# Opening of a fused LayerNorm, linear-attention and gated MLP kernel: idle products, the split of one load, and the order of a few products

## Chip, cores, metric

One core of one Trainium2 chip. The metric is the device time of one execution in microseconds; lower is better. A kernel is run several times, medians of fast runs are quoted, and executions of one kernel mostly differ by some tenths of a microsecond (those of before lay between 220.24 and 222.91 in all). "Landed" is the moment at which the profile has the last completion signal of a transfer.

## The reference

S = 2048 tokens of width 640, 32 heads of 20, MLP width 1728, all bf16:

```python
xn = layernorm(x)
q, k, v = split(xn @ wqkv)
pq, pk = phi(q), phi(k)                  # phi(t) = where(t > 0, t + 1, exp(t)) + 1e-6
o = (pq @ (pk^T v)) / (pq . sum(pk) + 1e-6)
s = o @ wo
g = silu(relu(xn @ w1) @ w2)
out = x + s * g
```

## The kernel before

The kernel is scheduled by hand: every operation is appended to the program of one engine (PE is TensorE, DVE VectorE, ACT ScalarE, POOL GpSimd, SP the queue of most transfers), and a small scheduler puts in the semaphore waits. Each engine is given its operations in the order in which they were appended, and the timelines below show PE, DVE and ACT starting them in that order. x comes in 16 tiles of 128 tokens. Only the opening, tiles 0 to 3, matters here. These tiles are centred by DVE (a mean half made by ACT, half by DVE, or all by ACT), transposed on PE, copied from PSUM to SBUF by DVE and ACT, and multiplied with the K columns of A_wqkv. `wqk` has five row pieces; `wk_load(k0, k1)` fetches pieces k0 to k1-1, and `K_mm(t, b, k0, k1)` appends the products of tile t with those pieces, two products of 320 columns per piece.

```python
zero = nc.alloc_sbuf_tensor("zero", [P, P], bf)
# [...]
sc.op("DVE", lambda eng: eng.memset(zero[:, :], 0.0), W=[("zero",)])
# [...]
x_load(0)                    # SP queue, 160 KB
x_load(1, 1, "ACT")          # ACT queue
wk_load(0, 2)                # SP, pieces one and two, 320 KB
x_load(2, 2, "ACT")          # ACT, tiles 2 and 3 in one transfer
wk_load(2, 3)                # SP, piece three, 160 KB
wk_load(3, 5)                # SP, pieces four and five
w1_load(0, "SP")
# [...]
def fill(n):                 # "idle products": their result is never read
    sc.group("PE", [(lambda eng: eng.matmul(ps[7][:, 0:P], lhsT=zero[:], rhs=zero[:], start=True, stop=True))
                    for _ in range(n)], R=[("zero",)], W=[("ps", 7)])
fill(31)
# [...]  the opening, in the order of each engine's program
bn(0, 0)                     # DVE, statistics of half of tile 0
mean_act(0, HN)              # ACT
half_mean_dve(0)
centre(0)                    # DVE
mean_act(1, 0)
transposes(0, 0)             # PE, five of 128x128
xcT_copy(0, 0, 0, "DVE")
centre(1)
fill(5)
K_mm(0, 2, 0, 1)             # tile 0, piece one
transposes(1, 6)
xcT_copy(0, 0, 1, "DVE")
bn(0, 1)                     # DVE, needed only for the scale used much later
mean_act(2, 0)               # ACT, waits for tile 2
xcT_copy(1, 6, 0, "DVE")
xcT_copy(1, 6, 1, "ACT")
K_mm(0, 2, 1, 3)             # tile 0, pieces two and three
K_mm(1, 4, 0, KA)            # tile 1, pieces one and two (KA = 2)
centre(2)
transposes(2, 0)
mean_act(3, HN)
bn(3, 0)
# [...]
K_mm(1, 4, 2, 3); K_mm(2, 6, 0, KA); K_mm(2, 6, 2, 3)
transposes(3, 0)
# [...]  22 more K products, then H blocks (products of 512 columns with w1)
```

## Time and profile before

| | before |
|---|---|
| median of the first 3 runs (range) | 220.86 us (220.54 to 221.12) |
| span of the profiled run | 219.3 us |
| PE busy | 214.5 us, 98% of the span |
| PE waits named in the whole span | 1.0 us, 0.6 us, 0.2 us |

The page gives the busy time of each engine with its share of the span, and the chain of work that ended last:

```profile
PE 214.5 (98%) x1451; PEld 133.7 (61%) x1461; DVE 119.1 (54%) x219; ACT 84.2 (38%) x140; POOL 43.8 (20%) x69
...
PE 95%; DMA 2%; DVE 1%; issue 0%; SPq 0%; ACT 0%; DVEq 0%
```

PE is the bound, and all other engines have room. What PE waited for, in total us, number of times and longest:

```profile
PE psT L384 <- DVE zero L356: 1.0, 1, 1.0
PE psT L493 <- DMA reg<-in_A_wqkv_dram: 0.6, 1, 0.6
PE psT L568 <- issue: 0.2, 1, 0.2
```

The second wait lies in the opening. PE's timeline there (start, length, line, how many, and in brackets the idle time before and what ended it; L384 are idle products, L468 transposes, L493 K products, L568 the H blocks):

```profile
1.04 3.49 PE L384 MATMUL psT<-zero 128*128 128x128 bf16 x31 [1.04 <-DVE zero L356]
4.43 0.79 PE L468 MATMUL psT<-ident,reg 128*128 128x128 bf16 x5
5.02 0.68 PE L384 MATMUL psT<-zero 128*128 128x128 bf16 x5
5.69 0.43 PE L493 MATMUL psT<-reg,regX 128*128 128x320 bf16 x2
5.96 0.44 PE L468 MATMUL psT<-ident,reg 128*128 128x128 bf16 x5
6.95 1.25 PE L493 MATMUL psT<-reg,regX 128*128 128x320 bf16 x8 [0.55 <-DMA reg<-in_A_wqkv_dram]
8.04 0.44 PE L468 MATMUL psT<-ident,reg 128*128 128x128 bf16 x5
8.31 1.37 PE L493 MATMUL psT<-reg,regX 128*128 128x320 bf16 x8
9.52 0.44 PE L468 MATMUL psT<-ident,reg 128*128 128x128 bf16 x5
9.80 3.15 PE L493 MATMUL psT<-reg,regX 128*128 128x320 bf16 x22
13.00 0.38 PE L568 MATMUL psT<-regX,reg 128*128 128x512 bf16 x1
```

The rate of the clock can be read from the spacing. The 31 idle products of 128 columns end at 4.53, 0.107 us apart; the five transposes that start at 5.96 are 0.056 us apart. The clock is at half rate first and is released at about 5.5 us. (The page's clock row shows full speed from the first slice on; the spacing says otherwise.) PE stands from about 6.40 to 6.95, and the chain says for what:

```profile
1.71 5.11 DMA reg<-in_A_wqkv_dram
6.82 0.14 issue
6.95 1.25 PE psT L493 x8
8.20 0.28 PE psT L468 x5
```

The third weight piece was issued at 1.71 and landed at 6.81. Tiles 2 and 3: ACT's timeline shows it idle for them until 6.45:

```profile
6.45 0.74 ACT L447 ACTIVATE regE<-reg 128x640 bf16<-128x640 bf16 x1 [1.92 <-DMA reg<-in_A_x_dram]
```

### The profile page before, as it was taken

The page shows a single profiled execution, that of the slowest core. Times are in us where ns is not written, and L with a number is a line of the kernel's source. Part 1 is how long each engine was busy: PE and PEld are TensorE (multiplying, and loading weights), DVE is VectorE, ACT ScalarE, POOL GpSimd, SP SyncE. Part 2 cuts the span into 40 slices and gives each one's busy share as a digit, 9 for nine tenths or more (in the row PEclk, how much of TensorE's full clock was granted, in tenths as well). Part 3 has the DMA queues.
Part 4 walks back from the last instruction along what each step waited for, and adds up shares of the span by engine and source line. Part 5 has one row for each costly group of instructions (what it writes and reads, how often), then busy time and mean ns, then how long its engine had stood idle before and what let it go on. Part 6 is the DMA issues. An engine that isn't in the chain of part 4 may idle for free.

```text
span 219.3 us, 3543 instructions
## 1 busy us (share of the span) xinstructions
PE 214.5 (98%) x1451; PEld 133.7 (61%) x1461; DVE 119.1 (54%) x219; ACT 84.2 (38%) x140; POOL 43.8 (20%) x69
## 2 busy tenths in 40 slices
PE   8899999999999999999999999999999999999995
PEld 7655554555545555444467777677767776777674
DVE  3798957789639999783702116930424240403134
ACT  5597675566665676554420000551021102110211
POOL 2178601120041699950000000000000000000001
PEclk9999999999999999999999999999999999999999
DMA  6977496711001243000099969932110100001011
GB/s 198 370 233 165 105 303 60 205 30 30 3 1 33 57 103 109 0 0 3 2 209 301 373 220 364 374 106 64 37 53 33 60 30 33 30 30 64 0 60 60
DMA packets 28421, 24.72 MB, mean 113 GB/s; under 512 B 12021, under 2 KB 27765, under 8 KB 28405
## 3 DMA queue, kind: packets, MB, share of 16 engines
q1 hardware_dynamic: 24677, 19.77, 31.7%
q10 hardware_dynamic: 3728, 4.73, 6.3%
q8 instruction: 11, 0.18, 0.4%
q14 instruction: 5, 0.04, 0.1%
HBM read 15.81 MB, written 5.24 MB: 96 GB/s over the span
## 4 chain that ended last, share of the span: by engine, by line
PE 95%; DMA 2%; DVE 1%; issue 0%; SPq 0%; ACT 0%; DVEq 0%
PE psT L849 26%; PE psT L568 25%; PE psT L493 10%; PE psT L789 10%; PE psT L546 10%; PE psT L900 9%; DMA reg<-in_A_wqkv_dram 2%; PE psT L867 1%; PE psT L587 1%; PE psT L819 1%; PE psT L804 1%; PE psT L676 0%; DVE reg L888 0%; ACT reg L877 0%; PE psT L468 0%
## 5 line engine op out<-in xcount | busy, mean ns | idle before, releaser
L849 PE MATMUL psT<-reg,hT 128*128 128x320 bf16 x416 | 60.5, 299 | 0.0
L849 PEld LDWEIGHTS psT<-reg,hT 128*128 128x128 bf16 x416 | 40.3, 98 | 16.4 <-issue 1.1
L568 PE MATMUL psT<-reg 128*128 128x512 bf16 x192 | 45.5, 379 | 0.3 <-issue 0.2
L888 DVE TENSOR_TENSOR reg<-psT,reg 128x640 bf16<-128x640 f32 (+2 forms) x18 | 13.3, 749 | 48.3 <-PE psT L900 47.1
L572 ACT ACTIVATE hT<-psT 128x512 bf16<-128x512 f32 x52 | 30.8, 602 | 18.0 <-PE psT L568 18.0
L568 PEld LDWEIGHTS psT<-reg 128*128 128x128 bf16 x195 | 18.9, 98 | 21.8 <-issue 0.4
L877 ACT ACTIVATE reg<-psT 128x640 bf16<-128x640 f32 x12 | 8.2, 702 | 44.7 <-PE psT L849 25.3
L893 POOL TENSOR_TENSOR reg<-reg 128x224 bf16<-128x224 bf16 x1 | 0.6, 606 | 120.3 <-DVE reg L888 120.3
L900 PE MATMUL psT<-reg,pqT 128*128 128x320 bf16 (+2 forms) x165 | 24.4, 295 | 0.0
L504 POOL TENSOR_TENSOR zacc<-zacc,reg 128x640 f32<-128x640 f32 x16 | 23.8, 1488 | 2.3 <-DVE reg L528 1.3
L546 PE MATMUL psT<-reg 128*128 128x512 bf16 x95 | 23.8, 379 | 0.3
L789 PE MATMUL psT<-reg 128*128 128x320 bf16 x160 | 21.9, 299 | 0.0
L900 PEld LDWEIGHTS psT<-reg,pqT 128*128 128x128 bf16 x165 | 16.1, 98 | 5.8
L789 PEld LDWEIGHTS psT<-reg 128*128 128x128 bf16 x160 | 15.7, 98 | 6.2
L510 ACT ACTIVATE regE<-psT 128x640 bf16<-128x640 f32 x24 | 15.6, 701 | 9.1 <-PE psT L493 9.1
L493 PE MATMUL psT<-reg 128*128 128x320 bf16 x120 | 18.3, 299 | 0.0
L554 DVE TENSOR_SCALAR regE<-psT 128x512 bf16<-128x512 f32 x20 | 13.6, 680 | 8.2 <-ACT regE L553 8.2
L556 DVE SCALAR_TENSOR_TENSOR pqT<-regE 128x512 bf16<-128x512 bf16 x20 | 17.4, 868 | 0.7
L546 PEld LDWEIGHTS psT<-reg 128*128 128x128 bf16 x100 | 9.8, 98 | 11.6
L493 PEld LDWEIGHTS psT<-reg 128*128 128x128 bf16 x120 | 11.7, 98 | 6.5 <-DMA reg<-reg 0.2
L794 DVE CAST reg<-psT 128x640 bf16<-128x640 f32 x5 | 4.1, 824 | 20.9 <-PE psT L789 20.9
L413 DVE BATCH_NORM_STATS2 stats<-reg 128x6 f32<-128x320 bf16 x32 | 14.1, 475 | 2.3 <-DMA reg<-in_A_x_dram 2.3
(69 smaller groups left out, 174.7 us busy)
## 6 DMA issues: line engine op xcount, KB each, us to landing
scr<-regE SPq DMA_DIRECT2D x4, 640.0 KB, 11.3
reg<-in_A_x_dram SPq DMA_DIRECT2D x4, 640.0 KB, 8.8
out_dram<-reg SPq DMA_DIRECT2D x15, 160.0 KB, 1.8
reg<-in_A_x_dram SPq DMA_DIRECT2D x13, 160.0 KB, 3.3
regE<-scr SPq DMA_DIRECT2D x4, 512.0 KB, 5.2
reg<-in_B_w_dram ACTq DMA_DIRECT2D x1, 1120.0 KB, 12.0
reg<-in_B_w_dram ACTq DMA_DIRECT2D x1, 1040.0 KB, 5.4
reg<-in_A_wo_dram SPq DMA_DIRECT2D x6, 160.0 KB, 4.6
```

The lines of the kernel that those rows point to most:

```text
L413: sc.op("DVE", lambda eng: eng.bn_stats(stats[:, t, a, :], xv[:, HN * a:HN * (a + 1)]), R=[("xin", t % XR)], W=[("stats", t, a)])
L493: fns.append(lambda eng, a=a, k=k, lhs=lhs: eng.matmul(ps[b + a][:, 0:HN], lhsT=lhs[:, k, tok(t)], rhs=wqk[:, k, D + HN * a:D + HN * (a + 1)],
L504: sc.op("POOL", lambda eng: eng.tensor_tensor(out=zacc[:, :], in0=zacc[:, :], in1=pk[:, t, :], op=ALU.add), R=[("zacc",), ("pk", t)], W=[( ...
L510: sc.op("ACT", lambda eng: eng.activation(out=o_.rearrange("p (a n) -> p a n", a=2), in_=ps2(b, HN), func=func, scale=scale), R=[("ps", b) ...
L546: sc.group("PE", [(lambda eng, k=k: eng.matmul(ps[b], lhsT=wqk[:, k, P * f:P * (f + 1)], rhs=xnT[:, k, schunk(j)], start=(k == 0), stop=(k ...
L554: sc.op("DVE", lambda eng: eng.tensor_scalar(out=r_, in0=ps[b], scalar1=0.0, scalar2=1e-6, op0=ALU.max, op1=ALU.add), R=[("ps", b), ("er_e ...
L556: sc.op("DVE", lambda eng: eng.scalar_tensor_tensor(out=pqT[:, f, schunk(j)], in0=e_, scalar=1.0, in1=r_, op0=ALU.min, op1=ALU.add), R=[(" ...
L568: a = sc.group("PE", [(lambda eng, k=k: eng.matmul(ps[b], lhsT=w1_sb[:, k, P * f:P * (f + 1)], rhs=src[:, k, :], start=(k == 0), stop=(k = ...
L572: sc.op("ACT", lambda eng: eng.activation(out=hT[:, f, schunk(j)], in_=ps[b], func=ACTF.Relu), R=[("ps", b)], W=[("hT", j, f)])
L789: fns.append(lambda eng, t=t, a=a: eng.matmul(ps[b + a][:, 0:HN], lhsT=xn[:, t, P * k:P * (k + 1)], rhs=pk[:, t, HN * a:HN * (a + 1)], sta ...
L849: sc.group("PE", [(lambda eng, f=f: eng.matmul(ps[b][:, 0:HN], lhsT=hT[:, f, tok(t)], rhs=w2_sb[:, f, HN * n:HN * (n + 1)], start=(f == 0 ...
L900: sc.group("PE", [(lambda eng, c=c: eng.matmul(ps[b][:, 0:hi - lo], lhsT=pqT[:, c, tok(t)], rhs=wf[:, c, lo:hi], start=(c == 0), stop=(c = ...
```

## The change

The intent is to fill the opening. Idle products read a constant that the framework sets up ahead of the program, so PE need not wait for DVE's memset. Tile 2 is loaded without tile 3, which goes behind the third weight piece on the other queue. The products with the third piece go behind four products that do not need it. The diff, whole:

```diff
-    zero = nc.alloc_sbuf_tensor("zero", [P, P], bf)
+    zero = nc.alloc_sbuf_tensor("zero", [P, 1], bf)
+    one = nc.const_aps.tensor(1.0, (P, P), bf)
@@
     x_load(0)
     x_load(1, 1, "ACT")
     wk_load(0, 2)
-    x_load(2, 2, "ACT")
+    x_load(2, 1, "ACT")
     wk_load(2, 3)
+    x_load(3)
     wk_load(3, 5)
@@
     def fill(n):
-        sc.group("PE", [(lambda eng: eng.matmul(ps[7][:, 0:P], lhsT=zero[:], rhs=zero[:], start=True, stop=True))
-                        for _ in range(n)], R=[("zero",)], W=[("ps", 7)])
+        sc.group("PE", [(lambda eng: eng.matmul(ps[7][:, 0:P], lhsT=one, rhs=one, start=True, stop=True))
+                        for _ in range(n)], W=[("ps", 7)])
@@
-    fill(31)
+    fill(32)
@@
     centre(1)
-    fill(5)
+    fill(3)
     K_mm(0, 2, 0, 1)
@@
-    K_mm(0, 2, 1, 3)
+    K_mm(0, 2, 1, KA)
     K_mm(1, 4, 0, KA)
+    K_mm(0, 2, 2, 3)
     centre(2)
```

## The prediction

> **What bounds the kernel now.** TensorE. The page's busy table gives PE 98% of a 219.3 us span, and the chain that ended last is PE for 95%. The waits of PE name three: 1.0 us at the start for the memset of `zero`, 0.55 us for a piece of A_wqkv before the matmuls at 6.95 us, and 0.2 us of issue. From 14 us on PE waits for no other engine. So only the first 9 us can change, and time saved there goes through whole to the end.
>
> **The opening, from the timeline.** The entry barrier ends at 0.72 us; the 31 idle products start at 1.04, 0.107 us apart, the cold clock's rate. K products of 320 columns come 0.136 us apart once warm, the first at 5.69. (The page's clock row shows full speed from the start; the spacing does not agree, and I trust the spacing.) Transposes of tile 0 start at 4.43, released by DVE's centring, not by the idle products. Five more idle products end at 5.55, where the first weight pieces also land, so tile 0's K products start at 5.69. PE stands from 6.40 to 6.95 for the third weight piece, landed 6.81; x tiles 2 and 3, one transfer, land at 6.42, and ACT had idled 1.92 us for them.
>
> **What the change does.**
> 1. Idle products start about 0.26 us earlier (0.78) and, being 32, end about 0.15 us earlier. Tile 0 is not ready before 4.43, so nothing is gained directly. The Trainium skill ("TensorE: Matmul & The Clock Gate", Part 1) says the clock is released by a busy window of about 3.4 us that runs free of the kernel; the earlier start moves the warm moment earlier by at most that 0.26 us on average. This trace agrees: warm about 4.4 us after the first product.
> 2. The x transfer on ACT's queue is halved. The skill ("DMA: Bandwidth & Descriptors", Queues, rings and completion order) says each engine takes packets of the queues in turn. At the 300 GB/s of the windows at 2 to 5 us, the 164 KB moved behind the third piece are 0.5 us: I estimate first two pieces at 5.2 (5.55), third at 5.8 to 6.2 (6.81), tile 2 near 5, tile 3 still near 6.4, pieces four and five unchanged near 7.6.
> 3. Two idle products fewer: 0.2 us of PE, which the earlier landing lets count.
> 4. Products that need the third piece go behind four that don't: the 0.55 us gap shrinks to at most 0.25, now for DVE's copy of tile 1.
>
> Walking the order again with these durations, the transposes of tile 3 start near 8.7 instead of 9.52: 0.6 to 0.9 us, all on PE's chain. Later needs keep margin: first part of w1 landed 9.39, needed about 12.2; transposed tile 4 landed 17.65, needed about 18.4.
>
> **Prediction.** 220.86 - 0.75 = 220.1 us, 8 in 10 between 219.4 and 220.7. Faster by over 2%: 0.01; within 2%: 0.98; slower: 0.01.
>
> **Signs.** PE's wait for A_wqkv gone or below 0.2 us; the first H block (512-column products) starts near 12.2 instead of 13.0; ACT's 1.92 us wait for x near 0.4; busy sums otherwise as before; PE still waits for nothing from 14 us on.
>
> **What would make it wrong.** A warm moment later relative to the start: the products at 5.4 to 7 us would run at half rate and the gain shrink or vanish. Tile 3 landing after 7.2 would hold DVE and ACT, which work in order. Reading a broadcast constant could be slower than a full tile. A later margin smaller than I read.

## The result

| | before | after |
|---|---|---|
| median of 6 runs (range) | 220.84 us (220.54 to 221.12) | 219.88 us (219.58 to 220.45) |
| span of the profiled run | 219.3 us | 218.3 us |
| PE busy | 214.5 us | 214.1 us |
| third weight piece landed | 6.81 us | 5.82 us |
| tile 2 landed | 6.42 us (with tile 3) | 5.22 us |
| transposes of tile 2 start | 8.03 us | 7.00 us |

The ratio is 0.9961 with a 95% interval of 0.9945 to 0.9976. A ratio here is the mean time of one kernel's fast runs over the mean of the other's fast runs of the same rounds, so it is not quite the ratio of the medians. The medians differ by 0.96 us.

The profile after, in the same views. The page:

```profile
PE 214.1 (98%) x1450; PEld 133.1 (61%) x1460; DVE 118.9 (54%) x219; ACT 84.2 (39%) x140; POOL 43.7 (20%) x69
...
PE 97%; DVE 1%; issue 0%; ACT 0%; DVEq 0%
```

PE's waits. The one for A_wqkv is gone; the first is only the entry barrier:

```profile
PE psT L386 <- PEq L994: 0.8, 1, 0.8
PE psT L570 <- issue: 0.2, 1, 0.2
```

PE's timeline (L386 idle products, L470 transposes, L495 K products, L570 H blocks):

```profile
0.82 3.57 PE L386 MATMUL psT<-const-bfloat16-1.0 128*128 128x128 bf16 x32 [0.82 <-PEq L994]
4.25 0.65 PE L470 MATMUL psT<-ident,reg 128*128 128x128 bf16 x5
4.73 0.34 PE L386 MATMUL psT<-const-bfloat16-1.0 128*128 128x128 bf16 x3
5.03 0.45 PE L495 MATMUL psT<-reg,regX 128*128 128x320 bf16 x2
5.33 0.45 PE L470 MATMUL psT<-ident,reg 128*128 128x128 bf16 x5
5.62 1.55 PE L495 MATMUL psT<-reg,regX 128*128 128x320 bf16 x8
7.01 0.44 PE L470 MATMUL psT<-ident,reg 128*128 128x128 bf16 x5
7.29 1.37 PE L495 MATMUL psT<-reg,regX 128*128 128x320 bf16 x8
8.49 0.44 PE L470 MATMUL psT<-ident,reg 128*128 128x128 bf16 x5
8.77 3.15 PE L495 MATMUL psT<-reg,regX 128*128 128x320 bf16 x22
11.98 1.46 PE L570 MATMUL psT<-regX,reg 128*128 128x512 bf16 x6
```

The idle products start at 0.82 instead of 1.04. The transposes of tile 1 start 0.63 us earlier (5.33), the K products that had stood at 6.95 start at 5.62, the transposes of tile 2 are 1.03 us earlier (7.01), and from there every line is earlier by 1.02 or 1.03 us. The gain is complete at 7 us, and nothing is given back later. (Some times in the tables are cut after the second decimal where the views round, so that a view can read 0.01 us more.) Not all of it need be the change: tile 0, whose transfer was not touched, landed at 3.04 us in this profile and at 3.23 in that of before, and over all profiles at 3.04 to 3.29. In all of them its transposes start 1.20 to 1.22 us after it landed, so 0.18 us of the 0.63 us for tile 1 was there before (4.43 to 4.25). ACT had idled 1.92 us for tile 2; it now idles 0.90:

```profile
5.24 0.74 ACT L449 ACTIVATE regE<-reg 128x640 bf16<-128x640 bf16 x1 [0.90 <-DMA reg<-in_A_x_dram]
```

PE still stands about 0.3 us inside its group of eight at 5.62: the second product starts at 5.75 and takes 0.136, the third starts at 6.18. The chain names DVE, whose statistics (L415) stand ahead of the copy that PE needs (L480):

```profile
5.53 0.40 DVE stats L415
5.93 0.20 DVE regX L480
...
6.18 0.99 PE psT L495 x6
```

### The profile page after: what moved, and what is told of

Same layout as the page of the kernel before. It is cut to its first block, busy times and chain, and to the rows that moved or that the text cites. A ratio compares the mean times of both kernels' runs of the same rounds, so it can differ in the third digit from the quotient of the medians.

```text
span 218.3 us, 3541 instructions
## 1 busy us (share of the span) xinstructions
PE 214.1 (98%) x1450; PEld 133.1 (61%) x1460; DVE 118.9 (54%) x219; ACT 84.2 (39%) x140; POOL 43.7 (20%) x69
## 3 DMA queue, kind: packets, MB, share of 16 engines
HBM read 15.81 MB, written 5.24 MB: 96 GB/s over the span
## 4 chain that ended last, share of the span: by engine, by line
PE 97%; DVE 1%; issue 0%; ACT 0%; DVEq 0%
PE psT L852 26%; PE psT L570 26%; PE psT L792 10%; PE psT L495 10%; PE psT L548 10%; PE psT L903 9%; PE psT L386 2%; PE psT L870 1%; PE psT L589 1%; PE psT L822 1%; PE psT L807 1%; PE psT L679 0%; DVE reg L891 0%; PE psT L470 0%; DVE regX L480 0%
## 5 line engine op out<-in xcount | busy, mean ns | idle before, releaser
L570 PE MATMUL psT<-reg 128*128 128x512 bf16 x192 | 45.5, 379 | 0.3 <-issue 0.2
L570 PEld LDWEIGHTS psT<-reg 128*128 128x128 bf16 x195 | 18.9, 98 | 21.9 <-issue 0.4
L495 PE MATMUL psT<-reg 128*128 128x320 bf16 x120 | 18.3, 299 | 0.0
L495 PEld LDWEIGHTS psT<-reg 128*128 128x128 bf16 x120 | 11.7, 98 | 6.5 <-DMA reg<-reg 0.2
L555 ACT ACTIVATE regE<-psT 128x512 bf16<-128x512 f32 x20 | 11.9, 597 | 8.8 <-PE psT L548 8.8
```

The costliest lines, as they stand in the source:

```text
L495: fns.append(lambda eng, a=a, k=k, lhs=lhs: eng.matmul(ps[b + a][:, 0:HN], lhsT=lhs[:, k, tok(t)], rhs=wqk[:, k, D + HN * a:D + HN * (a + 1)],
L570: a = sc.group("PE", [(lambda eng, k=k: eng.matmul(ps[b], lhsT=w1_sb[:, k, P * f:P * (f + 1)], rhs=src[:, k, :], start=(k == 0), stop=(k = ...
```

## The experiments

The gain lies in one pair of profiles, and in that pair several things differ: the landings, the place of the idle products, the order, and also the moment when the clock was released (about 5.5 before, 4.6 after). My theory, called the transfer theory, is that the landings of the third piece and of tile 2 held the opening and that splitting the load moved them. Its rivals: the clock theory (idle products from the first instruction release the clock earlier) and the order theory (moving the products fills PE's hole). Ten more kernels, and both kernels once again, were run in three calls, each call on one chip, beside the kernel before. All gave correct results.

One reading serves all: the start of the transposes of tile 3. In all fourteen profiles, the time of the run less that start lies between 211.03 and 211.10 us. So nothing after that point depends on what was changed, and each microsecond of the opening is a microsecond of the result. (I first used the first H block for this, and some of the expectations below name it. That was a poor mark: the trace of before has 192 products of that line against 195 weight loads, and in the early profiles the first product of the first H block is among the missing records, so that its start reads 0.2 us too late. The constant of 207.54 to 207.61 in an expectation below became 207.76 to 207.83 where the record was there.)

In the table, times are us from the start of the span. "Released" is the moment when 128-column products go from 0.107 to 0.056 us apart or 320-column ones from 0.267 to 0.136. "T" is the start of the transposes.

| kernel | pieces 1-2 landed | piece 3 | tile 2 | released | T tile 1 | T tile 2 | T tile 3 | that run, us |
|---|---|---|---|---|---|---|---|---|
| before | 5.55 | 6.81 | 6.42 | 5.5 | 5.96 | 8.03 | 9.52 | 220.57 |
| before, second profile | 4.80 | 7.31 | 7.48 | 6.7 to 7.4 | 6.11 | 8.81 | 10.30 | 221.33 |
| order only | 4.75 | 6.06 | 6.35 | 5.6 | 5.83 | 7.68 | 9.17 | 220.21 |
| idle products only | 5.29 | 6.58 | 6.13 | 5.7 | 5.90 | 7.80 | 9.29 | 220.35 |
| transfers only | 4.49 | 5.89 | 5.47 | 4.1 | 5.33 | 7.11 | 8.59 | 219.66 |
| after | 4.74 | 5.82 | 5.22 | 4.6 | 5.32 | 7.00 | 8.49 | 219.58 |
| after, second profile | 4.81 | 5.69 | 5.24 | 5.7 | 5.79 | 7.28 | 8.77 | 219.82 |
| after without the order | 4.92 | 5.73 | 5.29 | 4.0 | 5.42 | 6.95 | 8.43 | 219.49 |
| after without the idle products | 4.67 | 5.78 | 5.59 | 5.6 | 5.87 | 7.36 | 8.84 | 219.94 |
| after, 8 idle products | 4.74 | 5.65 | 5.21 | 7.7 | 5.93 | 8.16 | 9.64 | 220.71 |
| after, 2 and 3 behind piece 3 | 4.71 | 6.25 | 7.11 | 3.8 | 5.31 | 8.44 | 9.93 | 220.96 |
| after, order swapped | 5.08 | 5.71 | 5.27 | 5.2 | 5.56 | 6.96 | 8.45 | 219.51 |
| the same, statistics later | 4.67 | 5.69 | 5.10 | 5.6 | 5.72 | 7.09 | 8.57 | 219.63 |
| transfers and swapped order | 4.63 | 5.51 | 5.29 | 3.9 | 5.35 | 6.72 | 8.21 | 219.30 |

### Transfers only

```diff
 (kernel before)
-    x_load(2, 2, "ACT")
+    x_load(2, 1, "ACT")
     wk_load(2, 3)
+    x_load(3)
```

> The kernel before with only the transfers changed (x tiles 2 and 3 apart). Transfer theory (the third weight piece landed at 6.81 us because 164 KB of tile 3 shared the engines with it): the third piece lands near 5.9, the products of tile 0 with pieces two and three run without a hole at about 6.1, the transposes of tile 2 start near 7.2 (8.03 before) and the first H block near 12.2 (13.00); time 0.7 to 0.9 us below before. Clock theory (the gain is the earlier idle products): no gain, within 0.2 us. Order theory (the gain is the products moved back): no more than 0.3 us.

Measured: 219.66 us (219.54 to 219.83), before 220.89 (220.24 to 222.79), ratio 0.9943 (0.9913 to 0.9973). This part alone gives the whole gain: 1.23 us by the medians, where the whole change gave 0.96 in its call and I had expected 0.7 to 0.9. None of its six runs was as slow as the fastest of the eleven of before. The third piece landed at 5.89, and PE then waited for DVE and no longer for the weights; the transposes of tile 2 started at 7.11 (a line of PE's waits, then two of its timeline):

```profile
PE psT L494 <- DVE stats L414: 0.3, 1, 0.3
...
6.03 1.25 PE L494 MATMUL psT<-reg,regX 128*128 128x320 bf16 x8 [0.25 <-DVE stats L414]
7.11 0.44 PE L469 MATMUL psT<-ident,reg 128*128 128x128 bf16 x5
```

The clock and order theories, which expected at most 0.2 and 0.3 us, fall as explanations of the whole gain.

### Order only

```diff
 (kernel before)
-    K_mm(0, 2, 1, 3)
+    K_mm(0, 2, 1, KA)
     K_mm(1, 4, 0, KA)
+    K_mm(0, 2, 2, 3)
```

> The kernel before with only the products of the third piece moved back. Transfer theory: the hole before 6.95 shrinks to about 0.15 us, but tile 2 still lands at 6.4, so its transposes wait for DVE's centring until about 7.8; first H block near 12.75, gain 0.2 to 0.3 us. Order theory: the whole hole is won, 0.5 us or more. Clock theory: 0.

Measured: 220.64 us (220.21 to 221.41), ratio 0.9988 (0.9956 to 1.002). The medians differ by 0.25 us as the transfer theory said, but the interval holds 1. PE's wait for the weights is gone in this profile, and a wait for the centring of tile 2 stands in its place (the third piece also happened to land early, at 6.06, so this profile alone does not test the order):

```profile
PE psT L468 <- DVE reg L457: 0.2, 1, 0.2
```

### Idle products only

The edit takes the lines with `one`, `fill(32)` and `fill(3)` of the diff, and nothing else.

> The kernel before with only the idle products changed (on the constant, 32 from 0.8 us, 3 instead of 5 later). Transfer theory: 0 gain (within 0.15 us), since the third piece still lands at 6.8 and PE waits for it; the first H block at 13.0. Clock theory: 0.5 us or more, with the warm moment clearly earlier than in the kernel before.

Measured: 220.25 us (219.76 to 220.89), ratio 0.9969 (0.9937 to 1.0001). This is a miss of my number: 0.64 us by the medians where I had expected 0. The interval just touches 1. The profile does not show an effect of the idle products: PE still waits for the third piece, only less long because it landed at 6.58 and not at 6.81, and the clock was released no earlier than in before.

```profile
PE psT L494 <- DMA reg<-in_A_wqkv_dram: 0.4, 1, 0.4
```

So whether the idle products gain anything on the old transfers is not settled by this run.

### After without the order

```diff
 (kernel after)
-    K_mm(0, 2, 1, KA)
-    K_mm(1, 4, 0, KA)
-    K_mm(0, 2, 2, 3)
+    K_mm(0, 2, 1, 3)
+    K_mm(1, 4, 0, KA)
```

> The kernel after with the products of the third piece moved forward again. Transfer theory: the same as after within 0.1 us, first H block at 11.9 to 12.1, because the third piece has landed at 5.8 and in either order eight products lie between the transposes of tiles 1 and 2, with one hole of about 0.3 us. Order theory: 0.3 to 0.5 us slower than after.

Measured: 219.74 us (219.49 to 220.41), ratio 0.9951 (0.9916 to 0.9985), with transposes of tile 2 at 6.95 (7.00 in after). So the moved products bring the transposes of tile 2 no earlier once the load is split. The third piece had landed at 5.73, before the eight products started at 5.87.

### After with 8 idle products

The edit is `fill(8)` for `fill(32)` in the kernel after.

> The kernel after with 8 instead of 32 idle products at the start (same constant, same first instruction). If the clock matters in the opening at all: [...]the clock stays at half rate until at least 7.7 us, the K products from 5 us come 0.267 us apart instead of 0.136, first H block 1.5 to 3 us later than in after (11.98), time 1.5 to 3 us above after. If the warm moment is off the chain: within 0.2 us of after. With the run of the idle products alone this tells the worth of having them from that of starting them 0.2 us earlier.

Measured: 221.33 us (220.71 to 222.85), ratio 1.0026 (0.9986 to 1.0066) to before; after had 0.9961. That is 1.45 us above after's 219.88, which was on another chip, and 1.46 above the 219.87 that the kernel with the order swapped (below) had. I had expected 1.5 to 3 us; the profiled run, the fastest of the six, starts its first H block 1.15 us later than after (13.13). The clock stayed at half rate until 7.7 us, and the products at 5.40 and 6.46 show it:

```profile
5.40 0.74 PE L495 MATMUL psT<-reg,regX 128*128 128x320 bf16 x2
5.93 0.74 PE L470 MATMUL psT<-ident,reg 128*128 128x128 bf16 x5
6.46 1.86 PE L495 MATMUL psT<-reg,regX 128*128 128x320 bf16 x8
8.16 0.44 PE L470 MATMUL psT<-ident,reg 128*128 128x128 bf16 x5
```

Two K products take 0.74 us here and 0.45 in after; five transposes 0.74 and 0.45. So a stretch of idle products is worth having. That does not make a start 0.22 us earlier worth anything by itself.

### After with tiles 2 and 3 together, behind the third piece

```diff
 (kernel after)
-    x_load(2, 1, "ACT")
     wk_load(2, 3)
-    x_load(3)
+    x_load(2, 2)
```

> The kernel after with tiles 2 and 3 again one transfer, but on the queue of the weights, behind the third piece. Weights alone (what counted is only that the third piece lands earlier): as after, or 0.1 us better, the piece landing near 5.4. Both (tile 2 had to land early too, because ACT's mean and DVE's centring of it release the transposes of tile 2): tile 2 lands at 6.1 to 6.4, its transposes start near 7.6 (7.00 in after), first H block near 12.6, time 0.5 to 0.7 us above after.

Measured: 220.77 us (220.47 to 220.96), ratio 0.9984 (0.9954 to 1.0015). The gain of the change is gone. Tile 2 landed at 7.11, where I had put it at 6.1 to 6.4, and the chain runs from there through ACT's mean and DVE's centring to the transposes:

```profile
2.22 4.89 DMA reg<-in_A_x_dram
...
7.13 0.84 ACT regE L448 x2
...
8.00 0.40 DVE reg L458
...
8.44 0.45 PE psT L469 x5
```

So an earlier landing of the third piece alone (6.25 here) would not do. Tile 2 has to land early too, which is what taking tile 3 out of its transfer achieves. The reverse, tile 2 early with the third piece late, was not run.

### Order swapped, and with later statistics

```diff
 (kernel after; the second kernel takes both hunks)
     K_mm(0, 2, 1, KA)
-    K_mm(1, 4, 0, KA)
     K_mm(0, 2, 2, 3)
+    K_mm(1, 4, 0, KA)
@@ second kernel only
-    bn(0, 1)                 # ahead of mean_act(2, 0)
@@
+    bn(0, 1)                 # ahead of aggr(0)
     aggr(0)
```

> The kernel after with the two products of tile 0 on the third piece set before the four of tile 1, as a group of their own. In after PE stands from about 5.88 to 6.17 for DVE's copy of tile 1 although the third piece landed at 5.82. Chain theory: the two products fill this hole; transposes of tile 2 at about 6.73 (7.00), first H block near 11.7, 0.2 to 0.27 us below after. If something else held that stretch: no change.

> The same, and DVE's statistics of tile 0's second half moved from before the copy of tile 1 to before tile 0's aggregate. Chain theory: DVE's copy of tile 1 comes up to 0.2 us earlier, but with the swap PE is full between the transposes of tiles 1 and 2 already, so no more than 0.05 us beyond the swap; first H block near 11.7. If DVE's order is the bound instead of PE: 0.2 us more than the swap.

Measured: 219.87 us (219.43 to 220.17), ratio 0.9944 (0.9912 to 0.9976), and 219.95 us (219.32 to 220.44), ratio 0.9947 (0.9914 to 0.9979). The hole is gone as expected: the transposes of tiles 1 and 2 are 1.40 and 1.37 us apart, 1.68 in the profile of after. The statistics add nothing beyond, as expected. The start of the H block that I had named (11.7) was missed: in these two profiles the transposes of tile 1 came 0.24 and 0.40 us later than in after's, which took back what the swap gave. In the first this is the landing of tile 0 (3.27 for 3.04): from its transposes to those of tile 1 it is 1.08 us in both kernels, although the clock was released at 5.2 instead of 4.6. In the second tile 0 (3.21) accounts for 0.17 us; the other 0.23 goes with a release at 5.6.

### Second profiles of before and after

> The kernel before, unchanged, for a second profile of it. In all ten profiles so far the time of the run less the start of the first H block is 207.54 to 207.61 us, so a run's time can be read as that start plus 207.6. Expected if the third piece's landing (6.81 in the first profile) and tiles 2 and 3 (6.42) are what hold it: landings move by some tenths between runs, the first H block at 12.6 to 13.2, and the transposes of tile 2 about 1.2 to 1.4 us after the later of the two landings. If the first profile was an accident of a late clock: a run with the warm moment before 5 us starts the first H block before 12.4.

> The kernel after, unchanged, for a second profile and for times beside the others of this call. Expected: 0.8 to 1.1 us below before, first H block at 11.9 to 12.2; with a warm moment later than 5.2 us up to 0.2 us later than in its first profile (11.98).

Measured: before 220.70 us (220.25 to 221.33) and after 220.14 us (219.80 to 220.68), in a call where the runs of before had a median of 220.82. Their ratios to those runs are 0.9992 (0.9967 to 1.0016) and 0.9970 (0.9945 to 0.9995). So the gain of the whole change is 0.68 us by the medians here, less than the 0.8 to 1.1 that I had expected. In the second profile of before the third piece landed at 7.31 and tiles 2 and 3 at 7.48, the first H block started at 13.57 (expected 12.6 to 13.2), and the chain went through tile 2 instead of the weights:

```profile
1.45 6.03 DMA reg<-in_A_x_dram
...
7.50 0.84 ACT regE L447 x2
...
8.37 0.40 DVE reg L457
...
8.81 0.45 PE psT L468 x5
```

In the kernels with the old transfers and the old order of the products, the transposes of tile 2 start at the later of two times: the landing of tile 2 plus 1.33 us (7.48 + 1.33 = 8.81 here), or that of the third piece plus 1.22 us (6.81 + 1.22 = 8.03 in the first profile, 6.58 + 1.22 = 7.80 with the idle products alone). The first term holds in two more: 6.35 + 1.33 = 7.68 with the order alone, and 7.11 + 1.33 = 8.44 with tile 2 behind the third piece. Over the four profiles with the old transfers the third piece landed at 6.06 to 7.31, a range of 1.25 us; over the nine with the load split, at 5.51 to 5.89, of 0.38 us. That before's times spread more (220.24 to 222.91) would fit, but the landings are known for the profiled runs alone. The condition of a warm moment before 5 us did not occur in it.

### After without the idle products, and the best version

```diff
 (first kernel: after, with `zero` [P, P], fill(31) and fill(5) as in before)
 (second kernel: before, with)
-    x_load(2, 2, "ACT")
+    x_load(2, 1, "ACT")
     wk_load(2, 3)
+    x_load(3)
@@
-    K_mm(0, 2, 1, 3)
+    K_mm(0, 2, 1, KA)
+    K_mm(0, 2, 2, 3)
     K_mm(1, 4, 0, KA)
```

> The kernel after with the idle products of before (on the zeroed tile, 31 from 1.04 us, 5 later). If the idle products add nothing on top of the transfers: as after within 0.15 us, first H block at 12.0 to 12.2. If the two fewer idle products or the earlier start count: 0.2 to 0.4 us above after.

> The kernel before with the transfers changed and the products of the third piece as a group of their own straight after those of the second, no change of the idle products. Chain theory: no hole between the transposes of tiles 1 and 2 (1.37 to 1.40 us apart, 1.68 in after), so as after or up to 0.2 us below it; first H block at 11.8 to 12.1. If the idle products count on top: 0.2 us above the run with this order and the new idle products.

Measured: 219.88 us (219.62 to 219.94), ratio 0.9950 (0.9927 to 0.9973), and 219.60 us (219.30 to 219.84), ratio 0.9940 (0.9917 to 0.9963), against after's 220.14 and 0.9970. Taking the new idle products out of after did not make it slower. By the medians it was 0.26 us faster, which neither of my two cases had. The second kernel has the lowest median and the lowest single run (219.30, released at 3.9), 0.54 us below after by the medians, where I had expected up to 0.2; the ranges, 219.30 to 219.84 and 219.80 to 220.68, just overlap. Its transposes of tiles 1 and 2 are 1.36 or 1.37 us apart, with no hole:

```profile
5.36 0.44 PE L469 MATMUL psT<-ident,reg 128*128 128x128 bf16 x5
5.64 1.25 PE L494 MATMUL psT<-reg,regX 128*128 128x320 bf16 x8
6.72 0.44 PE L469 MATMUL psT<-ident,reg 128*128 128x128 bf16 x5
```

In the three pairs that differ in the idle products alone, the old ones were the faster each time by the medians: transfers only 219.66 against 219.74 with them, without them 219.88 against 220.14, swapped order 219.60 against 219.87. The runs above 220 us are all on the side of the new ones (five kernels, each with its slowest run between 220.17 and 220.68; the slowest without them is 219.94). The intervals of the ratios overlap in each pair, the third pair is from two chips, and the slow runs have no profile. Why it is so, and whether it would hold, stays open. The two fewer idle products before the first K products are a suspect that no run took apart, and the two profiles with a late clock (5.6 and 5.7) point the other way: from the transposes of tile 0 to the first K products it is 1.12 us in this kernel, with five idle products in between, and 0.90 in after's second profile, with three.

## Why the prediction was right

The time: 220.1 was forecast, between 219.4 and 220.7, and 219.88 came. The class, within 2%, was right. The sum of 0.75 us met 0.96 in the first and 0.68 in the second pair. The account of where it would come from was right in the main term and wrong in two others: 0.2 us were put down to the fewer idle products and 0.3 to the order, and neither could be shown to bring time. That the sum still came out is in part luck.

- *PE bounds all but the first 9 us, and time saved there goes through whole.* Right: run time less the start of the transposes of tile 3 is the same within 0.07 us in fourteen profiles.
- *The transfer of x on ACT's queue is halved, landings move.* Right, and it is the whole of the gain. Estimated and measured landings: pieces one and two 5.2 and 4.74; piece three 5.8 to 6.2 and 5.82; tile 2 near 5 and 5.22; tile 3 near 6.4 and 6.25; pieces four and five near 7.6 and 7.13. The Trainium skill's statement ("DMA: Bandwidth & Descriptors", Queues, rings and completion order) that the engines take the queues in turn agrees with the direction for the third piece and for tile 2, whose ranges with the old transfers (6.06 to 7.31 and 6.13 to 7.48) and with the load split (5.51 to 5.89 and 5.10 to 5.59) do not meet; no run here looks at single packets. For pieces one and two the ranges meet (4.75 to 5.55 and 4.49 to 5.08), so that landing is not shown to be the change's. Pieces four and five were forecast unchanged and came 0.5 us earlier than in before.
- *Idle products start 0.26 us earlier and gain nothing directly.* The start moved by 0.22 us (1.04 to 0.82). That the clock was released 0.9 us earlier in after's profile than in before's looked like an effect, and is not one: the release came at 3.9 and 4.1 with the old idle products and at 5.6 and 5.7 with the new ones in other profiles. The moment varies from run to run by more than the change moves it.
- *Two idle products fewer, "0.2 us of PE, which the earlier landing lets count".* Not shown as a gain: with the new idle products removed, after was not slower (219.88 against 220.14). The 0.2 us are there when the clock is late (1.12 and 0.90 us, above). With the clock released early, the first K products wait for DVE's copy of tile 0 and not for idle products. In after this copy ended at 4.97 and the products started at 5.03, while the idle products had ended streaming by 4.90.
- *"Products that need the third piece go behind four that don't: the 0.55 us gap shrinks to at most 0.25, now for DVE's copy of tile 1."* The gap of after is 0.29 us and it is DVE's copy, as said. But the order is not what shrank it: with the old order on the new transfers the transposes of tile 2 start at 6.95 against 7.00. Once the piece lands at 5.8, moving its products back leaves the hole open that they could have filled, and setting them first closes it.
- *Signs.* PE's wait for A_wqkv is gone, as forecast; the first recorded H product is at 11.98 (12.2); ACT's idle time is 0.90 us (0.4, a miss); PE waits for no other engine from 14 us on.
- *What would make it wrong.* A late clock was the right worry: among runs with the load split, a release at 5.6 to 5.7 put the transposes of tile 1 at 5.7 to 5.9, and one at 3.9 to 4.6 put them at 5.3 to 5.4. From the transposes of tile 0, which takes out the landing of tile 0, these are 1.31 to 1.48 and 0.97 to 1.08 us. It costs a few tenths, not the gain.

What stays open: whether the new idle products gain something on the old transfers (0.64 us by the medians, interval to 1.0001) or lose something on the new ones.

## What to carry to other kernels

When an engine waits for a transfer in the opening, look at what shares the transfer engines with it: bytes that are needed later, taken out of an early transfer and queued behind, brought forward both the weights and the tile. Undo each part of a bundled change by itself: three parts that each had a plausible share of the gain turned out to be one that had all of it and two that could not be shown to help. Before an effect is read from one pair of profiles, take a second profile of each; landings and the clock's release moved here by as much as the effect.

## What the Trainium skill lacked or had wrong

- "TensorE: Matmul & The Clock Gate", Part 1, gives a busy window of about 3.4 us before the clock is released. With the first product at 1.04 us the release came at 3.9 and 4.1 us in two profiles, 2.9 and about 3.1 us after it, so less than the page's window of products was enough there; whether the window was only partly busy or is shorter, these runs do not tell. With 8 idle products and PE otherwise idle until 4.49, it came at 7.7 us, 3.2 us after that.
- The same page, Part 2 (Back-to-back issue gap), gives about 81 ns per product of 128 columns for a stream in which each product has its own weight load. Here the transposes, five products of 128 columns with five weight loads, came 0.056 us apart, and products of 320 columns with a load each 0.136 us apart; the page's formula for the isolated gap, N / 2.4 + 2.5 ns, gives 0.056 and 0.136 and fits better than the figure for streams. Five products are a short stream, but the H blocks agree: their products of 512 columns, with a load each, came 0.216 us apart, where the page has about 131 ns for a stream and its formula gives 0.216.
- The same page, Part 4, says of PE transposes that the full clock "doesn't engage". The kernel's transposes (recorded as matmuls with the identity) ran 0.107 us apart before the release and 0.056 after it, so they do run at the full rate once the clock is released. Whether transposes alone would release it, no run shows.
- No page says by how much a landing varies when two queues are loaded at the start: the third piece landed anywhere from 6.06 to 7.31 us with the old transfers, and from 5.51 to 5.89 with the load split.
